# Fourier mixing and gated MLP in fp32: another place for one low part, one shift and eight turns, with more buffers for turns and outgoing rows

## The chip, the cores and the metric

The kernel runs on one core of a Trainium2 chip. The metric is device microseconds (us) of one execution; the time before is 964.4 us, the median of three runs.

## The reference

`x` is 2048 rows of 512, in fp32. All weights are given in fp32. `mod` is six vectors of 512 made from a condition `c`.

```python
sa, ca, ga, sb, cb, gb = (silu(c) @ w_mod) in six parts
h = layernorm(x) * (1 + ca) + sa
a, b = h @ dft_hid_re.T, h @ dft_hid_im.T
x = x + ga * (dft_seq_re @ a - dft_seq_im @ b)
h = layernorm(x) * (1 + cb) + sb                 # called h2 below
z = gelu(h @ w_in)                               # 512 -> 1792
z1, z2 = z[:, :896], layernorm(z[:, 896:])
out = x + gb * ((z1 * (w_sp @ z2 + b_sp)) @ w_out)
```

## The kernel before

**Three products for one.** Every fp32 matrix product is made of three products of a faster type: high part by high part, high by low, low by high (`matmul3`, L95 to L97). So each operand is split: ScalarE (ACT) copies the high part, VectorE (DVE) subtracts it to get the low part. For a moving block number n these are `prep_hi` (tile `ah`, L249) and `prep_lo` (tile `al`, L265). TensorE (PE) can't begin block n before `ah` n, nor its low product before `al` n. There are four buffers of `ah`, three of `al` and two of `t`, the block before the split.

**Stage 1**, blocks n = 0 to 127. A block is 128 x 512 of a sequence DFT matrix, loaded by SyncE (SP, L155) and turned on DVE (`squares`, L186). `mm_a(n)` does twelve matmuls with it against the 16 held row blocks of `h`. The blocks come in four groups t of 32; a group gives 512 output rows. Every 16 blocks four sums are split (`gh` on ACT L90, `gl` on DVE L91). Group t's sums go through the hidden DFT in four `mm_y(t, i)` of 24 matmuls, i = 0 to 3, each 128 rows. After each come:

- `post_y(t, i)`: DVE multiplies by `ga` (L546), adds x (L547), takes statistics (L103, L105); GpSimd (POOL) stores the rows (L548) and works out scale and shift (L107, L108, L115).
- `norm_y(t, i)`: ACT applies them (L119), which gives `h2`.
- `post_h(t, i)`: DVE multiplies by `1 + cb` (L557), POOL adds `sb` (L558).
- `turn_h(t, i)`: DVE turns 32 x 32 squares into a tile `hturn` (L564), of which there is one; POOL then issues four DMAs (L567) that write it to `ht_d[t]` in HBM.

**Stage 2a**, n = 128 to 155 (N2 = 128), makes the first half of `z` from `ht_d` by seven products of a Strassen-like scheme, two blocks n at a time (`mm_z1`, at even n). Its moving blocks lie in `xb` (groups 0 and 1 of `ht_d`, loaded near the end of stage 1) and `tt` (groups 2 and 3, loaded by SP at L205, at n = N2 and N2 + 3). Results are copied on ACT (`empty_z1`, L704) or finished with a gelu on ACT and a store by POOL (`end_z1`, L666 and L669) from rows `z1o`, of which there are three. **Stage 2b**, from N3 = 156, does the same for the second half (`mm_z2`, products emptied by DVE L742 and ACT). Then comes the long product with `w_sp` (`mm_w`, PSUM tiles `gw`), and the last one.

**Beside these**, blocks of `w_sp` are loaded (`load_s`, SP L761), summed on DVE in two steps one n apart (`sum_s`, L766 and L767, then L770 and L771) and stored (POOL L774) as operands of the long product.

**What sets the order.** Every engine runs its instructions in the order in which the program issues them. The program goes through n; before the block's matmuls `prep(n)` issues `ah` of n + 3 and `al` of n + 2, and behind them `run(n)` issues what `at(n, f, ...)` has put there by hand. So an `ah` stands behind all that ACT was given up to then, and so on. The last group's rows (t = 3) have no matmuls behind them in stage 1: their work is all put at N2 - 0.25, row after row, mixed with the first splits of the weights (`hi_v`, `lo_v`, `make_w7`, L606 and L614) and, ahead of row 2, with `prep(N2)`. Behind them `change_s()` closes the pools of stage 1 and opens `slots` in their place. Blocks n with n % 4 == 3 have their `al` in such a slot from N2 on, so `al` 131 (the low part of block N2 + 3) is issued after all turns of the last group.

```python
        if n % 2 == 0:
            prep_lo(n + 3)
        run(n)
        if n % 2 == 0:
            mm_z1(n)
```

Of the kernel before, what the change touches and what calls it, by code (L numbers as in the profile page):

```python
# [8 lines left out]
F32 = mybir.dt.float32  # L9
F32R = mybir.dt.float32r  # L10
AF = mybir.ActivationFunctionType
ALU = mybir.AluOpType

P = 128
# [5 lines left out]
def fnet_gmlp_kernel(  # L20
# [32 lines left out]
    nc = tc.nc  # L53
    S, D = x.shape[1:]
    F2 = w_in.shape[1]
    FH = F2 // 2
    Q = 512
    NQ = S // Q
# [7 lines left out]
    def pool(name, side="left", bufs=1):  # L66
        return tc.tile_pool(name=name, bufs=bufs, side=side, reuse_waits="tile")
# [55 lines left out]
    def at(n, f, *a):  # L123
        fill.setdefault(n, []).append((f, a))
# [14 lines left out]
    N2 = 4 * len(src)  # L139
    YPROD = (1, 2, 6, 7, 4, 5, 3)  # L140
    NY = {p: N2 + 4 * i for i, p in enumerate(YPROD)}
    N3 = N2 + 4 * len(YPROD)
# [7 lines left out]
    stage, T, AH, AL = {}, {}, {}, {}  # L150
# [39 lines left out]
    def prep(n):  # L190

        if n not in prepared:
            prepared.add(n)
            prep_hi(n + 3)
            prep_lo(n + 2)

    def slot(i, name, dtype=F32):
        return slots[0].tile([P, Q], dtype, tag=f"slot{i}", bufs=1, name=name)

    slots, TT, S2, XH = [], {}, {}, {}  # L200
# [55 lines left out]
    def prep_lo(n):  # L256
        if n >= NE or n in lows:
            return
        lows.add(n)
        if N2 <= n < N4 and n % 4 == 3:  # L260
            AL[n] = slot(0, f"al{n}", F32R)
        else:
            AL[n] = blocks.tile([P, Q], F32R, tag="al", bufs=3, name=f"al{n}")
        t = T.pop(n)
        nc.vector.tensor_tensor(AL[n], t, AH[n].bitcast(F32), op=ALU.subtract)  # L265
        gg, kk = divmod(n % 4, 2)
        if NY[6] <= n < NY[6] + 4:
            nc.vector.tensor_tensor(TT[kk, gg], TT[kk, gg], S2[gg, kk], op=ALU.add)
        elif NY[7] <= n < NY[7] + 4:
            nc.vector.tensor_tensor(TT[2 + kk, gg], TT[2 + kk, gg], S2[gg, kk], op=ALU.subtract)  # L270
# [4 lines left out]
    rows = p2.enter_context(pool("rows", "right"))  # L275
    s1 = ctx.enter_context(ExitStack())
    spool = s1.enter_context(pool("spool", "right"))
    GP_ = []
# [13 lines left out]
    wm, mods = {}, {}  # L292
# [262 lines left out]
    def post_h(t, i):  # L555
        h2 = LN.pop((t, i))
        nc.vector.tensor_tensor(h2, h2, mods[4], op=ALU.mult)  # L557
        nc.gpsimd.tensor_tensor(h2, h2, mods[3], op=ALU.add)  # L558
        LN[t, i] = h2

    def turn_h(t, i):
        h2 = LN.pop((t, i))
        ht = GP_[0].tile([P, D], F32, tag="hturn", bufs=1, name=f"hturn{t}_{i}")
        nc.vector.transpose(ht.rearrange("p (b i) -> p b i", i=32), h2.rearrange("p (b i) -> p b i", i=32))  # L564
        v = ht_d[t].rearrange("(b c) (a i r) -> a i c b r", c=32, a=4, i=4)
        for a in range(4):
            nc.gpsimd.dma_start(v[a, i], ht[32 * a:32 * a + 32].rearrange("c (b r) -> c b r", r=32))  # L567


    ZT = {}  # L570
# [76 lines left out]
    def mm_f7(g, k, th, tl):  # L647

        if k == 0:
            ZT["f7", g] = bank(6 + g % 2, f"f7p{g}")  # L650
        matmul3(ZT["f7", g], W7[0][:, 0, k], W7[0][:, 1, k], th, tl, k == 0, k == ND - 1)
        if k == ND - 1:
            end_z1(g, NF - 1, ZT.pop(("f7", g)), out_row(g, NF - 1))

    def out_row(g, f, tag="z1o"):
        return zrow[0].tile([P, Q], F32, tag=tag, bufs=3 if tag == "z1o" else 6, name=f"z1o{g}_{f}")

    def natural(z):
        return z.rearrange("p (a k i) -> p k a i", a=4, i=32)
# [39 lines left out]
    def empty_z1(p, gg, f):  # L699

        ps = ZT[gg, f]
        if p in (1, 6, 7):
            Z1[p, gg, f] = zrow[0].tile([P, Q], F32, tag="z1u" if p == 6 else "z1m", bufs=6, name=f"z1_{p}_{gg}{f}")
            nc.scalar.activation(natural(Z1[p, gg, f]), turned(ps), AF.Copy)  # L704
        elif p in (2, 4):
            g, f = gg, f + (3 if p == 4 else 0)
            end_z1(g, f, ps, out_row(g, f, "z1u" if p == 2 else "z1o"))
        else:
            z = Z1.pop((7 if p == 5 else 6, gg, f))
            nc.vector.tensor_tensor(natural(z), turned(ps), natural(z), op=ALU.add)  # L710
            end_z1(2 + gg, f + (3 if p == 5 else 0), None, z)
# [233 lines left out]
    norm_x(1)  # L945
    lo_h(0)
    prep_lo(0)
    hi_h(1)
    prep_hi(1)
    stats_x(2)  # L950
    lo_h(1)
    prep_lo(1)
    norm_x(2)
    prep_hi(2)
# [40 lines left out]
    for j, turn, weigh, row, fold, hi in ((0, (25, 26, 27, 28), (29, 29, 30, 30), 26, (34, 34, 35, 36), (38, 35, 36, 37)),  # L995
# [8 lines left out]
        n = weigh[3] + (3 if j == 0 else 1)  # L1004
# [4 lines left out]
            at(hi[k], make_ht, j, k)  # L1009
            at(hi[k] + 1, make_ht_lo, j, k)  # L1010
    for j, load_at, n, m, k, plus_one in ((2, 41, 49, 50, 7, False), (4, 52, 56, 58, 7, True),
                                          (3, 60, 65, 66, 7, False), (5, 68, 74, 76, 6, False)):
        at(load_at, load_mod, j)
        at(n, sum_mod, j, [0, 1])
        at(m, sum_mod, j, [2, 3])
        at(m + 1, split_mod, j)
        at(m + 3, spread_mod, j, k, cpool if j == 5 else htpool, plus_one)
    for t in range(NQ):
        n = 8 * NQ * (t + 1)
        for i in range(4):  # L1020
            y = N2 - 1 if t == NQ - 1 else (54, 56, 58, 60)[i] if t == 0 else n + (7, 9, 11, 13)[i] if t == 1 else n + 1 + 3 * i
            if i < 2:
                at(y - 4, load_xr, t, i)
            if t == 0:
                at((41, 42, 43, 45)[i], mm_y, t, i, (0,))
                at((42, 43, 44, 46)[i], keep_y, t, i)
            at(y, mm_y, t, i, (0, 1) if t else (1,))
            if t < NQ - 1:
                at(y + 1, post_y, t, i)
                at(y + 2, norm_y, t, i)  # L1030
                at(y + 3 if t else 71 + i, post_h, t, i)
                at(y + 4 if t else 72 + 2 * i, turn_h, t, i)
                if i < 2:
                    at(y + 2 if t else y + 3, load_xr, t, i + 2)
            else:
                if i == 2:
                    at(N2 - 0.25, prep, N2)
                at(N2 - 0.25, post_y, t, i)
                at(N2 - 0.25, norm_y, t, i)
                if i:  # L1040
                    at(N2 - 0.25, turn_h, t, i - 1)
                at(N2 - 0.25, post_h, t, i)
                if i < 2:
                    at(N2 - 0.25, load_xr, t, i + 2)
                for f, *a in (((hi_v, 1), (lo_v, 1)), ((make_w7, 0),), ((hi_v, 2), (lo_v, 2), (make_w7, 1)), ((turn_h, t, 3),))[i]:
                    at(N2 - 0.25, f, *a)
# [8 lines left out]

    wstack = ctx.enter_context(ExitStack())
    w0 = ctx.enter_context(ExitStack())
    wpool, zpool, zrow, bpool, spre, gpool = [], [], [], [], [], []
    at(N2 - 0.5, change_w)
    def change_s():  # L1060
        p2.close()
        slots.append(ctx.enter_context(pool("slots", "right")))
        spre.append(ctx.enter_context(pool("spre", "right")))
        bpool.append(ctx.enter_context(pool("bpool", "right")))
# [3 lines left out]
        spre.append(hp.enter_context(pool("spre0")))  # L1068

    at(80, change_q)  # L1070
    when = [(82 + 4 * i, 3) for i in range(11)] + [(N2 + 6, 8), (N2 + 14, 8), (N2 + 22, 8), (N3 + 4, 6), (N3 + 10, 6)]
    for (n, m), u in zip(when, ((r, g, b) for g in range(2) for b in range(4) for r in range(2))):
        at(n, load_s, *u)
        at(n + m, sum_s, *u, True)
# [6 lines left out]
        run(n + 0.75)  # L1081

    change_s()
    at(N2, load_t, 2)
    at(N2 + 1, load_wi, 1, 0)
    at(N2 + 1, load_wi, 1, 2)
# [35 lines left out]
    for i, p in enumerate(PROD):  # L1122
        for k in range(8):
            n = NB[p] + 2 * k
# [10 lines left out]
    for f in range(NF):  # L1135
        n = N4 + 24 + 8 * f
# [107 lines left out]
```

## Time and profile before

| | |
|---|---|
| median of 3 runs | 964.4 us (963.7 to 964.64) |
| profiled execution, its own time | 961.22 us |
| its span, first to last instruction | 959.4 us |
| mean granted TensorE clock | 0.992 |
| instructions | 12378 |
| PE, DVE, ACT, POOL busy | 936.5, 738.0, 413.6, 204.4 us |

The profile is one execution. A busy time is the sum over an engine's instructions; an engine that is not busy waits for another engine, for a DMA, or has nothing left. In a timeline row the first number is the start, the second the duration (of all, where x3 or x4 stands), and a bracket at its end gives the idle time of the engine ahead of it and who ended it. `Lnn` is the line in the kernel before. In the changed kernel the same lines stand 2 to 4 lines lower from L564 on (L564 is L565, L567 is L569, L666 is L670, L704 is L708, L742 is L746).

### The profile page before, as it was taken

The page shows a single profiled execution, that of the slowest core. Times are in us where ns is not written, and L with a number is a line of the kernel's source. Part 1 is how long each engine was busy: PE and PEld are TensorE (multiplying, and loading weights), DVE is VectorE, ACT ScalarE, POOL GpSimd, SP SyncE. Part 2 cuts the span into 40 slices and gives each one's busy share as a digit, 9 for nine tenths or more (in the row PEclk, how much of TensorE's full clock was granted, in tenths as well). Part 3 has the DMA queues.
Part 4 walks back from the last instruction along what each step waited for, and adds up shares of the span by engine and source line. Part 5 has one row for each costly group of instructions (what it writes and reads, how often), then busy time and mean ns, then how long its engine had stood idle before and what let it go on. Part 6 is the DMA issues. An engine that isn't in the chain of part 4 may idle for free.

```text
span 959.4 us, 12378 instructions
## 1 busy us (share of the span) xinstructions
PE 936.5 (98%) x4114; PEld 774.2 (81%) x4114; DVE 738.0 (77%) x1197; ACT 413.6 (43%) x725; POOL 204.4 (21%) x378
## 2 busy tenths in 40 slices
PE   8999999999999999999599999999999999999998
PEld 5888888888877888888487898788888888888886
DVE  7799957785668677866586859999799889886662
ACT  4694424232132221321485867766545454332221
POOL 2330000113663165325513301332000000000000
PEclk9999999999999999999799999999999999999999
DMA  9996652666348977994575413453465455744451
GB/s 210 220 222 131 128 141 62 172 176 154 107 119 238 320 215 211 279 333 160 185 268 197 198 44 88 112 152 88 111 142 138 105 135 123 192 92 161 178 178 61
DMA packets 235600, 157.07 MB, mean 164 GB/s; under 512 B 130448, under 2 KB 202384, under 8 KB 235408
## 3 DMA queue, kind: packets, MB, share of 16 engines
q1 hardware_dynamic: 223008, 118.65, 49.8%
q0 software_dynamic: 12192, 37.24, 10.9%
q8 instruction: 32, 0.52, 0.2%
q10 hardware_dynamic: 336, 0.39, 0.1%
q14 instruction: 32, 0.26, 0.1%
HBM read 119.54 MB, written 36.70 MB: 163 GB/s over the span
## 4 chain that ended last, share of the span: by engine, by line
PE 48%; DVE 2%; ACT 1%; POOL 1%; DMA 1%; issue 1%; DVEq 0%; POOLq 0%; ACTq 0%
PE gw L97 10%; PE gw L95 9%; PE gw L96 9%; PE op L95 3%; PE op L96 3%; PE op L97 3%; PE z1p L96 2%; PE z1p L97 2%; PE z1p L95 2%; PE z2p L97 2%; PE z2p L96 2%; PE z2p L95 2%; DMA ht_d<-hturn 1%; DVE al L265 1%; DVE z L742 0%
## 5 line engine op out<-in xcount | busy, mean ns | idle before, releaser
L249 ACT ACTIVATE ah<-t 128x512 fp32r<-128x512 f32 x248 | 156.4, 631 | 373.3 <-DVE t L186 259.6
L265 DVE TENSOR_TENSOR al<-t,ah 128x512 fp32r<-128x512 f32 x248 | 167.4, 676 | 64.0 <-PE gp L96 38.0
L95 PE MATMUL gp<-ah,hh 128*128 128x512 f32 x496 | 193.7, 391 | 2.4 <-DVE gl L91 2.4
L96 PE MATMUL gp<-al,hh 128*128 128x512 f32 x496 | 193.8, 391 | 1.7 <-DVE al L265 1.7
L97 PE MATMUL gp<-ah,hl 128*128 128x512 f32 x496 | 193.5, 390 | 0.0
L186 DVE STREAM_TRANSPOSE t<-stage 128x512 f32<-128x512 f32 x240 | 168.7, 703 | 8.4 <-DMA stage<-in_A_dft_seq_re_dram 3.6
L97 PE MATMUL gw<-ah,bl 128*128 128x512 f32 x400 | 155.8, 390 | 0.3 <-DVE bl L802 0.3
L95 PE MATMUL gw<-ah,bh 128*128 128x512 f32 x400 | 155.7, 389 | 0.0
L96 PE MATMUL gw<-al,bh 128*128 128x512 f32 x400 | 155.6, 389 | 0.0
L95 PEld LDWEIGHTS gp<-ah,hh 128*128 128x128 f32 x496 | 93.4, 188 | 22.4 <-DVE gl L91 2.8
L96 PEld LDWEIGHTS gp<-al,hh 128*128 128x128 f32 x496 | 93.5, 188 | 21.5 <-DVE al L265 2.2
L97 PEld LDWEIGHTS gp<-ah,hl 128*128 128x128 f32 x496 | 93.6, 189 | 19.4
L97 PEld LDWEIGHTS gw<-ah,bl 128*128 128x128 f32 x400 | 75.1, 188 | 16.5 <-DVE bl L802 1.0
L96 PEld LDWEIGHTS gw<-al,bh 128*128 128x128 f32 x400 | 75.1, 188 | 15.6
L95 PEld LDWEIGHTS gw<-ah,bh 128*128 128x128 f32 x400 | 75.1, 188 | 15.5
L774 POOL DMA_DIRECT2D s_d<-sj x64 | 35.2, 550 | 114.3 <-DVE sj L766 97.5
L95 PE MATMUL yp<-hth,gh 128*128 128x512 f32 x128 | 49.8, 389 | 0.0
L96 PE MATMUL yp<-htl,gh 128*128 128x512 f32 x128 | 49.8, 389 | 0.0
L97 PE MATMUL yp<-hth,gl 128*128 128x512 f32 x128 | 49.8, 389 | 0.0
L567 POOL DMA_DIRECT2D ht_d<-hturn x64 | 42.2, 665 | 31.1 <-DVE hturn L564 25.9
L95 PE MATMUL op<-woh,uh 128*128 128x512 f32 x112 | 43.6, 389 | 0.0
L96 PE MATMUL op<-wol,uh 128*128 128x512 f32 x112 | 43.6, 389 | 0.0
(199 smaller groups left out, 1451.0 us busy)
## 6 DMA issues: line engine op xcount, KB each, us to landing
stage<-in_A_dft_seq_im_dram SPq DMA_DIRECT2D x64, 256.0 KB, 5.1
sj<-in_B_w_sp_dram SPq DMA_DIRECT2D x32, 512.0 KB, 7.4
s_d<-sj POOLq DMA_DIRECT2D x64, 256.0 KB, 4.1
stage<-s_d SPq DMA_DIRECT2D x128, 128.0 KB, 2.8
stage<-in_A_dft_seq_re_dram SPq DMA_DIRECT2D x60, 256.0 KB, 5.5
stage<-in_B_w_sp_dram SPq DMA_DIRECT2D x96, 128.0 KB, 3.1
wm<-in_w_mod_dram SPq DMA_DIRECT2D x16, 256.0 KB, 5.6
xr<-in_A_x_dram POOLq DMA_DIRECT2D x16, 256.0 KB, 4.4
```

Source lines behind the costliest of these rows:

```text
L95: nc.tensor.matmul(acc, ah, bh, start=first, stop=False, skip_group_check=go_on)
L96: nc.tensor.matmul(acc, ah, bl, start=False, stop=False, skip_group_check=go_on)
L97: nc.tensor.matmul(acc, al, bh, start=False, stop=last, skip_group_check=go_on)
L186: nc.vector.transpose(dst.rearrange("p (b i) -> p b i", i=32), block[:, :, 32 * k:32 * k + 32])
L249: nc.scalar.activation(AH[n], T[n], AF.Copy)
L265: nc.vector.tensor_tensor(AL[n], t, AH[n].bitcast(F32), op=ALU.subtract)
L567: nc.gpsimd.dma_start(v[a, i], ht[32 * a:32 * a + 32].rearrange("c (b r) -> c b r", r=32))
L774: nc.gpsimd.dma_start(s_d[m, r, g][b * P:(b + 1) * P, :], a)
```

## The change

There are seven edits.

1. `al` 131 is issued inside the last group's rows, behind `post_y(3, 3)`, and lies in a buffer of the ring `z1u` (six rows of the pool `z1rows`) instead of a slot.
2. `sb` is added on DVE instead of POOL for the last group.
3. Turns (3, 1) and (3, 3) go into buffers of the ring `row` (six) instead of the one `hturn`.
4. Of turn (3, 3)'s four DMAs the last two are issued by ACT.
5. The rows `z1o` get a pool of their own with seven buffers, instead of three.
6. The vector `sb` (mod 3) is summed at n = 63 and 64 instead of 65 and 66; `post_h(0, i)` stands at 68 + i instead of 71 + i; the turns of group 0 stand at 69, 71, 73, 75 instead of 72, 74, 76, 78, those of group 1 at 77, 80, 82, 84 instead of 75, 77, 79, 81.
7. The last five `load_s` stand at N2 + 6, 14, 20, 26 and 32, each with its sums 8 and 9 behind, instead of N2 + 6, 14, 22 (8 and 9 behind) and N3 + 4, N3 + 10 (6 and 7 behind).

```diff
         if N2 <= n < N4 and n % 4 == 3:
-            AL[n] = slot(0, f"al{n}", F32R)
+            AL[n] = slot(0, f"al{n}", F32R) if slots else zrow[0].tile([P, Q], F32R, tag="z1u", bufs=6, name=f"al{n}")
...
     def post_h(t, i):
-        nc.gpsimd.tensor_tensor(h2, h2, mods[3], op=ALU.add)
+        (nc.vector if t == NQ - 1 else nc.gpsimd).tensor_tensor(h2, h2, mods[3], op=ALU.add)
...
     def turn_h(t, i):
-        ht = GP_[0].tile([P, D], F32, tag="hturn", bufs=1, name=f"hturn{t}_{i}")
+        pl, tag, n = (rows, "row", 6) if t == NQ - 1 and i % 2 else (GP_[0], "hturn", 1)
+        ht = pl.tile([P, D], F32, tag=tag, bufs=n, name=f"hturn{t}_{i}")
...
-            nc.gpsimd.dma_start(v[a, i], ht[32 * a:32 * a + 32].rearrange("c (b r) -> c b r", r=32))
+            eng = nc.scalar if (t, i) == (NQ - 1, 3) and a > 1 else nc.gpsimd
+            eng.dma_start(v[a, i], ht[32 * a:32 * a + 32].rearrange("c (b r) -> c b r", r=32))
...
     def out_row(g, f, tag="z1o"):
-        return zrow[0].tile([P, Q], F32, tag=tag, bufs=3 if tag == "z1o" else 6, name=f"z1o{g}_{f}")
+        if tag == "z1o":
+            return zout[0].tile([P, Q], F32, tag=tag, bufs=7, name=f"z1o{g}_{f}")
+        return zrow[0].tile([P, Q], F32, tag=tag, bufs=6, name=f"z1o{g}_{f}")
...
-                                          (3, 60, 65, 66, 7, False), (5, 68, 74, 76, 6, False)):
+                                          (3, 60, 63, 64, 7, False), (5, 68, 74, 76, 6, False)):
...
-                at(y + 3 if t else 71 + i, post_h, t, i)
-                at(y + 4 if t else 72 + 2 * i, turn_h, t, i)
+                at(y + 3 if t else 68 + i, post_h, t, i)
+                at(y + 4 if t > 1 else (69 + 2 * i, (77, 80, 82, 84)[i])[t], turn_h, t, i)
...
                 at(N2 - 0.25, post_y, t, i)
+                if i == 3:
+                    at(N2 - 0.25, prep_lo, N2 + 3)
                 at(N2 - 0.25, norm_y, t, i)
...
-    when = [(82 + 4 * i, 3) for i in range(11)] + [(N2 + 6, 8), (N2 + 14, 8), (N2 + 22, 8), (N3 + 4, 6), (N3 + 10, 6)]
+    when = [(82 + 4 * i, 3) for i in range(11)] + [(N2 + d, 8) for d in (6, 14, 20, 26, 32)]
...
     change_s()
+    zout.append(w0.enter_context(pool("zout")))
```

**Around `al` 131 on DVE**, at the end of stage 1. The rows of before start with the last row's `post_y(3, 3)`; `h2_3_3` is its `h2`, and the number behind a name only tells buffers apart.

```order
L546 TENSOR_TENSOR y3_3_4220<-yp3_3_0_4099,mod2_1784 128x512
L547 TENSOR_TENSOR xr3_3_4183<-y3_3_4220,xr3_3_4183 128x512
L103 BN_STATS bsty_4224<-xr3_3_4183 128x6
L105 BN_AGGR mvy_4226<-bsty_4224 128x2
L564 STREAM_TRANSPOSE hturn3_2_4235<-h2_3_2_4205 128x512
L557 TENSOR_TENSOR h2_3_3_4233<-h2_3_3_4233,mod4_2060 128x512
L564 STREAM_TRANSPOSE hturn3_3_4243<-h2_3_3_4233 128x512
L265 TENSOR_TENSOR al131_4261<-xb0_3845,ah131_4188 128x512
L265 TENSOR_TENSOR al132_4312<-xb1_3935,ah132_4305 128x512
```

The same place on DVE in the changed kernel:

```order
L546 TENSOR_TENSOR y3_3_4220<-yp3_3_0_4099,mod2_1784 128x512
L547 TENSOR_TENSOR xr3_3_4183<-y3_3_4220,xr3_3_4183 128x512
L103 BN_STATS bsty_4224<-xr3_3_4183 128x6
L105 BN_AGGR mvy_4226<-bsty_4224 128x2
L265 TENSOR_TENSOR al131_4233<-xb0_3845,ah131_4188 128x512
L565 STREAM_TRANSPOSE hturn3_2_4237<-h2_3_2_4205 128x512
L557 TENSOR_TENSOR h2_3_3_4235<-h2_3_3_4235,mod4_2060 128x512
L558 TENSOR_TENSOR h2_3_3_4235<-h2_3_3_4235,mod3_2222 128x512
L565 STREAM_TRANSPOSE hturn3_3_4245<-h2_3_3_4235 128x512
L265 TENSOR_TENSOR al132_4315<-xb1_3935,ah132_4308 128x512
```

`al` 131 moved up past both turns and the multiplication between them, and one addition (L558) came in ahead of the last turn.

**On ACT at the same place**, in the changed kernel; before, the same rows stand there without the DMAs:

```order
L119 ACTIVATE h2_3_3_4235<-xr3_3_4183,nmry_4231,rsy_4228 128x512
L569 DMA ht_d3_83<-hturn3_3_4245 32x16x32 x2
L708 ACTIVATE z1_1_00_4302<-z1p1_00_4274 128x4x4x32
L708 ACTIVATE z1_1_01_4304<-z1p1_01_4281 128x4x4x32
L708 ACTIVATE z1_1_02_4306<-z1p1_02_4288 128x4x4x32
L249 ACTIVATE ah132_4308<-xb1_3935 128x512
L249 ACTIVATE ah133_4313<-xb1_3935 128x512
```

The two DMAs stand ahead of three copies of a product (L708) and of `ah` 132, the high part that PE needs first for the pair N2 + 4.

**On DVE in stage 1**, around n = 80. Before, with `t` and `al` the blocks' turns and low parts, `gl2_0` the low parts of the sums:

```order
L186 STREAM_TRANSPOSE t82_2666<-stage20_2341 128x512
L265 TENSOR_TENSOR al81_2670<-t81_2627,ah81_2629 128x512
L91 TENSOR_TENSOR gl2_0_0_2685<-gp2_0_0_2141,gh2_0_0_2684 128x512
L91 TENSOR_TENSOR gl2_0_1_2689<-gp2_0_1_2142,gh2_0_1_2688 128x512
L91 TENSOR_TENSOR gl2_0_2_2693<-gp2_0_2_2143,gh2_0_2_2692 128x512
L91 TENSOR_TENSOR gl2_0_3_2697<-gp2_0_3_2144,gh2_0_3_2696 128x512
L564 STREAM_TRANSPOSE hturn1_2_2705<-h2_1_2_2600 128x512
L186 STREAM_TRANSPOSE t83_2713<-stage20_2341 128x512
L265 TENSOR_TENSOR al82_2722<-t82_2666,ah82_2668 128x512
L557 TENSOR_TENSOR h2_1_3_2711<-h2_1_3_2711,mod4_2060 128x512
L186 STREAM_TRANSPOSE t84_2746<-stage21_2530 128x512
L265 TENSOR_TENSOR al83_2750<-t83_2713,ah83_2715 128x512
```

In the changed kernel, from behind `gl2_0` on:

```order
L186 STREAM_TRANSPOSE t83_2701<-stage20_2359 128x512
L265 TENSOR_TENSOR al82_2710<-t82_2660,ah82_2662 128x512
L565 STREAM_TRANSPOSE hturn1_1_2728<-h2_1_1_2503 128x512
L557 TENSOR_TENSOR h2_1_3_2699<-h2_1_3_2699,mod4_2060 128x512
L186 STREAM_TRANSPOSE t84_2740<-stage21_2536 128x512
L265 TENSOR_TENSOR al83_2744<-t83_2701,ah83_2703 128x512
L186 STREAM_TRANSPOSE t85_2758<-stage21_2536 128x512
L265 TENSOR_TENSOR al84_2762<-t84_2740,ah84_2742 128x512
L565 STREAM_TRANSPOSE hturn1_2_2776<-h2_1_2_2600 128x512
L186 STREAM_TRANSPOSE t86_2785<-stage21_2536 128x512
L265 TENSOR_TENSOR al85_2789<-t85_2758,ah85_2760 128x512
L186 STREAM_TRANSPOSE t87_2803<-stage21_2536 128x512
```

Turn (1, 1) now comes behind `gl2_0` where (1, 2) came, and (1, 2) and (1, 3) follow two blocks apart each, instead of (1, 3) alone.

More of the change, by code (lines that the diff above doesn't have):

```diff
@@ L1057, in fnet_gmlp_kernel @@
     w0 = ctx.enter_context(ExitStack())
-    wpool, zpool, zrow, bpool, spre, gpool = [], [], [], [], [], []
+    wpool, zpool, zrow, zout, bpool, spre, gpool = [], [], [], [], [], [], []
     at(N2 - 0.5, change_w)
```

## Prediction

> **What bounds the kernel now.** I read the page's busy times first, then the waits of PE, then PE's timeline around each wait.
>
> ```profile
> PE 936.5 (98%) x4114; PEld 774.2 (81%) x4114; DVE 738.0 (77%) x1197; ACT 413.6 (43%) x725; POOL 204.4 (21%) x378
> ```
>
> PE is busy for 98% of the span. No edit takes a matmul away, so all there is to gain or lose is PE's idle time and the slow clock that may follow it. The waits of PE (us in total, times, longest):
>
> ```profile
> PE z1p L96 <- DVE al L265: 9.7, 1, 9.7
> PE gp L95 <- DVE gl L91: 2.4, 1, 2.4
> PE gp L96 <- DVE al L265: 1.7, 1, 1.7
> ...
> PE z2p L95 <- ACT ah L249: 1.4, 1, 1.4
> ...
> PE f7p L95 <- ACT ah L249: 0.4, 1, 0.4
> ```
>
> Three places matter. **B**, the largest, is where stage 2a begins; PE's timeline there:
>
> ```profile
> 460.53 0.39 PE L95 MATMUL z1p<-ah,vj 128*128 128x512 f32 x1
> 470.59 0.80 PE L96 MATMUL z1p<-al,vj 128*128 128x512 f32 x1 [9.67 <-DVE al L265]
> 471.18 0.63 PE L97 MATMUL z1p<-ah,vj 128*128 128x512 f32 x1
> ...
> 474.30 0.40 PE L96 MATMUL z1p<-al,vj 128*128 128x512 f32 x1
> ...
> 476.82 0.39 PE L95 MATMUL f7p<-ah,w 128*128 128x512 f32 x1
> ```
>
> From 474.30 to 476.82 stand 11 steps from matmul to matmul: 0.229 us each, the normal pace. From 460.53 to 474.30 there are 10 steps, which at that pace take 2.3 and took 13.8: a loss of 11.5. Of it 9.7 is the wait and 1.8 the slower steps behind it (0.63 long in the row of 471.18, where the others are 0.39).
>
> **A** is in stage 1, around n = 80 and 86:
>
> ```profile
> 275.08 0.39 PE L97 MATMUL gp<-ah,hl 128*128 128x512 f32 x1
> 277.83 0.50 PE L95 MATMUL gp<-ah,hh 128*128 128x512 f32 x1 [2.35 <-DVE gl L91]
> ...
> 282.97 0.39 PE L95 MATMUL gp<-ah,hh 128*128 128x512 f32 x1
> ...
> 291.26 0.50 PE L96 MATMUL gp<-al,hh 128*128 128x512 f32 x1 [1.74 <-DVE al L265]
> ```
>
> From 275.08 to 282.97 are 16 steps: 7.9 instead of 3.7, a loss of 4.2, of which 2.35 is the wait and 1.6 the slow clock (0.25 or so is the restart). The second wait costs 1.74 and a restart, 2.0, with no slow steps behind it. A loses 6.2. **C** is the small rest in stage 2: the 0.4 and 1.4 of the list, with 0.2 and restarts beside the first, about 2.8.
>
> **B after the change.** What PE waits for is `al` 131, which ends a row of work on DVE:
>
> ```profile
> 450.30 1.78 DVE L265 TENSOR_TENSOR al<-xb,ah 128x512 fp32r<-128x512 f32 x1
> 452.01 0.68 DVE L546 TENSOR_TENSOR y<-yp,mod 128x512 f32<-128x512 f32 x1
> 452.72 1.07 DVE L547 TENSOR_TENSOR xr<-y,xr 128x512 f32<-128x512 f32 x1
> ...
> 458.53 2.03 DVE L614 TENSOR_TENSOR w<-w,w 128x256 fp32r<-128x256 f32 x1
> 460.48 0.68 DVE L546 TENSOR_TENSOR y<-yp,mod 128x512 f32<-128x512 f32 x1
> 461.19 0.69 DVE L547 TENSOR_TENSOR xr<-y,xr 128x512 f32<-128x512 f32 x1
> ...
> 462.65 0.18 DVE L105 BATCH_NORM_AGGREGATE mvy<-bsty 128x2 f32<-128x6 f32 x1
> ...
> 465.01 0.69 DVE L557 TENSOR_TENSOR h<-h,mod 128x512 f32<-128x512 f32 x1 [0.34 <-ACT h L119]
> 469.26 0.71 DVE L564 STREAM_TRANSPOSE hturn<-h 128x512 f32<-128x512 f32 x1 [3.55 <-DMA ht_d<-hturn]
> 469.89 1.85 DVE L265 TENSOR_TENSOR al<-xb,ah 128x512 fp32r<-128x512 f32 x3
> ```
>
> The last row's statistics end at 462.83, but `al` 131 stands behind two turns, the second of them held 3.55 us by the DMAs of the turn before, which still read the one `hturn`. Issued behind the statistics it would start there. But the addition now comes in on DVE for each of the rows 0 to 2 ahead of it: 3 x 0.73 us (0.69 as L557, and the step to the next). Against that, DVE instructions with two inputs are long wherever POOL's addition runs beside them:
>
> ```profile
> 458.97 1.29 POOL L558 TENSOR_TENSOR h<-h,mod 128x512 f32<-128x512 f32 x1
> ```
>
> L614 takes 2.03 beside this one (its sibling of the same size, with no POOL work beside it, should take a half of the 0.69 of a 512-wide one, some 0.4), `al` takes 1.78 against 1.85 / 3 = 0.62, and L547 takes 1.07 twice against 0.69. Lifted, these give back 1.6 + 1.1 + 0.4 + 0.4 = 3.5. All of them lie on a chain that passes through POOL and ACT, so not all of it arrives: bounds are 0 and 3.5, less 2.2 spent. I take nearly the upper end, since the longest two stand directly in DVE's row ahead of a `y`: `post_y(3, 3)` starts at 460.48 - 1.3 = 459.2. Its statistics end 2.35 later, at 461.55, and `al` 131 ends at 462.2. PE is ready for it at 460.92, so a wait of **1.3** is left of 9.67.
>
> A new wait is next. The pair N2 + 4 needs `ah` 132 from ACT after 20 more matmuls (470.59 to 476.82 in the rows above), 20 x 0.229 = 4.6 us later: at 466.8. ACT's rows there:
>
> ```profile
> 464.16 0.81 ACT L119 ACTIVATE h<-xr,nmry,rsy 128x512 f32<-128x512 f32 x1 [6.24 <-POOL nmry L115]
> 464.88 1.55 ACT L704 ACTIVATE z<-z1p 128x512 f32<-128x512 f32 x3
> 466.32 1.16 ACT L249 ACTIVATE ah<-xb 128x512 fp32r<-128x512 f32 x2
> ```
>
> L119 starts 1.33 after the statistics' end (464.16 - 462.83), so at 462.9, and ends at 463.7. DVE then multiplies, adds and turns, 0.7 + 0.73 + 0.71: turn (3, 3) ends at 465.85, with nothing to hold it, as its buffer is another. Only then can ACT issue its two DMAs, and the three copies and `ah` 132 stand behind them. What such a DMA costs on ACT only one group of rows shows:
>
> ```profile
> L376 ACTq DMA_DIRECT2D x<-in_A_x_dram x4: 429/442/443, 0.7 to 2.1; - x4
> ```
>
> That is 0.44 us for rows of another shape; on POOL one of these takes 0.67 (2.68 / 4, below). I take 0.44, and keep 0.67. The DMAs are out at 466.75, the copies at 468.3, `ah` 132 at 468.9: a wait of **2.1**, and 0.4 more for `al` 132 (0.62 behind it, against one step of PE). So 3.8 of waits, 0.5 of restarts, and the slow clock: the nearest wait, 2.35 us, brought 1.6, the one of 1.74 nothing. I count 1.6 once. B then loses 5.9 instead of 11.5: **5.6 gained**.
>
> [...]
>
> The other readers of the turns are not late. POOL issues the four DMAs of turn (3, 2) behind `al` 131 and then two of (3, 3):
>
> ```profile
> 464.96 2.68 POOL L567 DMA_DIRECT2D ht_d<-hturn  x4 [0.83 <-DVE hturn L564]
> ...
> 471.49 2.58 POOL L567 DMA_DIRECT2D ht_d<-hturn  x4 [2.56 <-DVE al L265]
> ```
>
> From 462.9 six of them end at 466.9, where before the last ended at 474.07. `tt` of group 3 is loaded behind that, so it comes some 7 us earlier than now.
>
> **A after the change.** DVE's turns are held by the DMAs of the turn before:
>
> ```profile
> 271.68 0.71 DVE L564 STREAM_TRANSPOSE hturn<-h 128x512 f32<-128x512 f32 x1 [3.51 <-DMA ht_d<-hturn]
> ...
> 289.33 0.71 DVE L564 STREAM_TRANSPOSE hturn<-h 128x512 f32<-128x512 f32 x1 [6.18 <-DMA ht_d<-hturn]
> ```
>
> The first hold, of 3.51, stands just ahead of the `gl` that PE waited 2.35 for. In the changed order turn (1, 1) stands behind them and (1, 0) three blocks ahead, as mod 3's earlier sum lets group 0 turn three blocks earlier. I take this wait and its slow clock as gone: 4.2. The price comes behind it: turns (1, 1), (1, 2), (1, 3) now stand two blocks apart, 24 matmuls or 5.5 us, and each takes four issues (2.7) and the landing. Two windows show the landing, the first at 251 to 255 us beside a block's load, the other at 261 to 264 without:
>
> ```profile
> ht_d<-hturn POOLq DMA_DIRECT2D x4, 64.0 KB, 5.9
> ```
> ```profile
> ht_d<-hturn POOLq DMA_DIRECT2D x4, 64.0 KB, 2.1
> ```
>
> So a turn follows the one before by 4.8 to 8.6 us against 5.5. Here, beside loads of blocks and of `w_sp`, the longer is the nearer: the second turn is held about 3.1, the third up to 6. A hold of 6.18 cost PE 1.74, so DVE runs some 4.4 ahead. The second's hold fits in that, nearly (0.3); the third finds DVE's lead regained and costs about 1.7 as now. With restarts A loses 2.5 instead of 6.2: **3.7 gained** (bounds 6.2, with short landings, and -1, if the third adds 2.4 and a slow clock).
>
> **C after the change.** ACT's gelu into `z1o` is held by the store of an earlier row, and DVE's sums of `w_sp` stand among the emptying of `z2p`:
>
> ```profile
> 517.16 0.60 ACT L666 ACTIVATE z1o<-z1p 128x512 f32<-128x512 f32 x1 [2.77 <-DMA z_d<-z1o]
> ```
> ```profile
> 576.91 0.68 DVE L766 TENSOR_TENSOR sj<-sj 128x512 f32<-128x512 f32 x1
> ```
>
> Seven buffers end the hold; PE's waits of 0.4 and 0.2 with their restarts, 1.0, go. Four sums of 0.7 move away from 577 to 582, four blocks earlier, where they stand beside the first products of stage 2b and may cost 0.4; of the 1.4 wait at the end I take 1.2 as gone. **1.8 gained**, between -0.5 and 2.8.
>
> **Sum.** 5.6 + 3.7 + 1.8 = 11.1 off the profiled execution's 961.2: 950.1. That execution lies 3.2 below the median of 964.4, so the forecast is 953.3 us.
>
> **The rivals.** *More is gained.* No slow clock at B (1.6), landings of 2.1 in A (2.5 more), C in full (0.5 more): 953.3 - 4.6 = 948.7. For it speaks that the wait of 1.74 brought no slow clock; against, that the landing beside a block's load was 5.9.
>
> *Less is gained.* The lifted holds pay nothing, since the chain through POOL and ACT sets the rows' pace, and the three additions stay: `post_y(3, 3)` at 462.7, `al` 131 at 465.7, a wait of 4.8 with a slow clock, then 0.9 for `ah` 132 and `al` 132, with restarts 7.8: 3.7 gained. If A's third turn queues at the same time, its gain is nothing, and so C's: 964.4 - 3.7 = 960.7. For it speaks that ACT's L119, which stands ahead of the multiplication, waits for POOL's constants (6.24 in its row), and not for DVE's room. If A loses its 1 besides, and C its 0.5, it ends near no change.
>
> *Slower.* ACT, in order, stands behind turn (3, 3): the turn's new buffer in `row` is the one that held `xr` of row (3, 2), and is free only when that row's store by POOL, among the loads, has landed. Each us that the turn ends later than 465.85 is a us on `ah` 132. The gains in A and C pay for 5.5 of them, B's for 5.6, and the bound of 0.2% is 1.9: from a turn at 478.9 on it is slower. At 481 the time is 953.3 + 15 = 968. Against it stands the row of that store's issue; the landing would have to take over 20 us:
>
> ```profile
> 454.09 0.56 POOL L548 DMA_DIRECT2D x_d<-xr  x1 [0.31 <-DVE xr L547]
> ```
>
> **Chances.** Forecast 0.58, more 0.18, less 0.18 (of which 0.05 within 0.2%), slower 0.06. A change of 0.2%, 1.9 us, is about what a measurement of this kernel can tell from none. So faster 0.89, within 0.2% 0.05, slower 0.06. The range reaches from 946.5 (below the better case, by C's and A's bounds) to 961.
>
> **What would show it.** Right: the wait of z1p L96 for `al` falls from 9.7 to 1 or 2; a new wait for `ah` of about 2 stands at the pair N2 + 4, with ACT's two DMA issues ahead of it; gp L95 for `gl` is gone from the list; the last hold of a turn by `ht_d` stays near 6 us, and gp L96 for `al` near 2. The 2.77 of `z1o` is gone. Wrong: if DVE's `y` of the last row starts at 462 or later, the lifted holds paid nothing; if turns (1, 2) and (1, 3) show holds over 8, A is worse than counted; if ACT idles beyond 478 for the last turn, the slower case holds.

## The result and the profile after

| | before | changed |
|---|---|---|
| median | 964.05 us, 4 runs (962.89 to 964.64) | 950.62 us, 4 runs (949.74 to 951.59) |
| profiled execution | 961.22 us | 949.74 us |

The ratio is 0.9862, 95% interval 0.9845 to 0.9879: 1.4% faster. The two profiled executions differ by 11.5 us, where the forecast had 11.1. Of all executions in this document one, of the run E10 below, is left out: it took 2437.94 us, where the nine others took 957.25 to 963.16.

The waits of PE in the changed kernel (us in total, times, longest):

```profile
PE f7p L95 <- ACT ah L249: 2.3, 1, 2.3
PE z2p L95 <- ACT ah L249: 1.7, 2, 1.4
...
PE z1p L96 <- DVE al L265: 1.0, 1, 1.0
PE gp L96 <- DVE al L265: 0.9, 1, 0.9
```

The 9.7 for `al` 131 is 1.0, the 2.4 for `gl` has left the list, and a new 2.3 for `ah` stands on top. PE's timeline at B:

```profile
455.86 0.39 PE L95 MATMUL z1p<-ah,vj 128*128 128x512 f32 x1
457.21 0.50 PE L96 MATMUL z1p<-al,vj 128*128 128x512 f32 x1 [0.96 <-DVE al L265]
...
461.69 0.39 PE L97 MATMUL f7p<-ah,w 128*128 128x512 f32 x1
464.39 0.49 PE L95 MATMUL f7p<-ah,w 128*128 128x512 f32 x1 [2.31 <-ACT ah L249]
465.11 0.79 PE L96 MATMUL f7p<-al,w 128*128 128x512 f32 x1 [0.23 <-DVE al L265]
465.70 0.63 PE L97 MATMUL f7p<-ah,w 128*128 128x512 f32 x1
...
468.58 0.40 PE L95 MATMUL z1p<-ah,vj 128*128 128x512 f32 x1
```

From 455.86 to 468.58 there are 30 steps. At 0.229 us they take 6.9; they took 12.7. B loses 5.9 (12.72 less 6.87), where it lost 11.5. Who made `ah` 132 late is read on DVE and then on ACT:

```profile
454.23 0.68 DVE L546 TENSOR_TENSOR y<-yp,mod 128x512 f32<-128x512 f32 x1
...
456.50 0.66 DVE L265 TENSOR_TENSOR al<-xb,ah 128x512 fp32r<-128x512 f32 x1
...
460.55 0.71 DVE L565 STREAM_TRANSPOSE hturn<-h 128x512 f32<-128x512 f32 x1
464.37 1.29 DVE L265 TENSOR_TENSOR al<-xb,ah 128x512 fp32r<-128x512 f32 x2 [3.10 <-ACT ah L249]
```
```profile
458.25 0.81 ACT L119 ACTIVATE h<-xr,nmry,rsy 128x512 f32<-128x512 f32 x1 [5.56 <-POOL nmry L115]
461.30 0.91 ACTq L569 DMA_DIRECT2D ht_d<-hturn  x2
462.25 1.57 ACT L708 ACTIVATE z<-z1p 128x512 f32<-128x512 f32 x3 [3.18 <-PE f7p L97]
463.69 1.16 ACT L249 ACTIVATE ah<-xb 128x512 fp32r<-128x512 f32 x2
```

ACT has nothing to do from 459.1 to 461.3. The bracket of the 462.25 row puts its 3.18 us of idle time down to PE, but the matmuls of that product were long done: the row above shows that two DMA issues stood ahead in ACT's order, and they started when the turn had ended at 461.26. `ah` 132 is the first of two at 463.69.

In A two turns are still held, and PE's wait behind the second is short:

```profile
285.70 0.71 DVE L565 STREAM_TRANSPOSE hturn<-h 128x512 f32<-128x512 f32 x1 [4.84 <-DMA ht_d<-hturn]
...
292.82 0.71 DVE L565 STREAM_TRANSPOSE hturn<-h 128x512 f32<-128x512 f32 x1 [3.92 <-DMA ht_d<-hturn]
```
```profile
294.75 0.50 PE L96 MATMUL gp<-al,hh 128*128 128x512 f32 x1 [0.91 <-DVE al L265]
```

### The profile page after: what moved, and what is told of

It is laid out like the page before. It is cut to its first block, busy times and chain, and to the rows that moved or that the text cites. A ratio compares the mean times of both kernels' runs of the same rounds, so it can differ in the third digit from the quotient of the medians.

```text
span 948.0 us, 12382 instructions
## 1 busy us (share of the span) xinstructions
PE 934.8 (99%) x4114; PEld 773.2 (82%) x4114; DVE 737.5 (78%) x1201; ACT 413.5 (44%) x725; POOL 196.2 (21%) x372
## 4 chain that ended last, share of the span: by engine, by line
PE 86%; issue 6%; POOL 3%; DVE 3%; ACT 1%; DMA 1%; SPq 0%; POOLq 0%; DVEq 0%
PE gp L96 12%; PE gp L95 12%; PE gp L97 12%; PE gw L97 10%; PE gw L96 10%; PE gw L95 10%; PE op L97 3%; PE op L96 3%; PE op L95 3%; PE yp L97 2%; PE yp L96 2%; PE yp L95 2%; PE z2p L97 2%; PE z2p L96 2%; PE z2p L95 2%
```

## The experiments

Each ratio is to the kernel before, run beside it on the same chip; the changed kernel's is 0.9862. The kernel before took 963.1 to 965.1 us (medians) beside the different groups of runs, so two changed kernels are compared by their ratios, of which 0.001 is 0.96 us. Where two profiles are compared "matmul by matmul", it is by the start of the same matmul in both.

| | edit | median us | ratio, 95% interval |
|---|---|---|---|
| E1 | without edit 4 (POOL issues the last turn's DMAs) | 947.22 | 0.9816 (0.9798 to 0.9833) |
| E2 | without edit 2 (addition on POOL) | 955.42 | 0.9898 (0.9881 to 0.9915) |
| E3 | without edit 1 (`al` 131 late) | 953.59 | 0.9887 (0.9868 to 0.9906) |
| E4 | without edit 6 (turns of groups 0 and 1) | 956.27 | 0.9908 (0.9892 to 0.9923) |
| E5 | without edit 5 (three rows `z1o`) | 952.79 | 0.9887 (0.9872 to 0.9902) |
| E6 | without edit 7 (late sums) | 950.15 | 0.9857 (0.9839 to 0.9874) |
| E7 | without edit 3 (one `hturn`) | 955.32 | 0.9915 (0.9899 to 0.9932) |
| E8 | E1, turns (1, 2), (1, 3) later | 944.87 | 0.9804 (0.9789 to 0.9819) |
| E9 | before with edit 1 alone | 957.75 | 0.9942 (0.9922 to 0.9962) |
| E10 | before with edit 6 alone | 959.17 | 0.9960 (0.9942 to 0.9978) |
| E11 | E8 without edit 7 | 944.60 | 0.9810 (0.9786 to 0.9834) |

### E1: the last turn's DMAs on POOL

```diff
-            eng = nc.scalar if (t, i) == (NQ - 1, 3) and a > 1 else nc.gpsimd
+            eng = nc.gpsimd
```

> Edit 4 undone alone: POOL issues all four DMAs of the last turn, so nothing on ACT waits for the turn. Theory (ACT, in order, held ah 132 back): ACT has its three copies and ah 132 done 2.2 us after L119, that is before PE asks for it; only al 132, behind the turn on DVE, is left, a wait of 0.2 or so. The wait of 2.3, the slow steps behind it and the restart go, 4.5 us in all: about 946 us. Rival (the last rows of h2 reach HBM in time only because two queues issue them): their last issue comes 1.3 us later, the load of group 3 with it, and its first reader on ACT holds the products behind it: PE gets a new wait at the second or third pair, and the time stays at 950 or is above.

By the ratios the kernel is 4.4 us faster than the changed one (3.4 by the medians). On ACT and DVE nothing of the product stands behind the turn any more:

```profile
459.31 0.81 ACT L119 ACTIVATE h<-xr,nmry,rsy 128x512 f32<-128x512 f32 x1 [5.55 <-POOL nmry L115]
460.03 1.55 ACT L708 ACTIVATE z<-z1p 128x512 f32<-128x512 f32 x3
461.47 1.15 ACT L249 ACTIVATE ah<-xb 128x512 fp32r<-128x512 f32 x2
```
```profile
461.61 0.71 DVE L565 STREAM_TRANSPOSE hturn<-h 128x512 f32<-128x512 f32 x1
462.25 1.25 DVE L265 TENSOR_TENSOR al<-xb,ah 128x512 fp32r<-128x512 f32 x2
```

`ah` 132 is made while the last turn is still to come, and the wait of 2.3 has gone; a wait of 0.3 further on, for a gelu of ACT, is new. The theory holds: matmul by matmul PE gains 4.6 us in B and gives 0.4 back at the new wait, so the two DMA issues on ACT, 0.91 us of ACT's own time, cost about 4 us through what stood behind them. The rival's wait for the load of group 3 isn't there. The profiled execution is only 2.4 us below the changed kernel's. In A, where the kernel is the same, PE waited 2.33 instead of 0.91, and the old wait of 1.44 near the end of stage 2b was followed by a slow spell, which cost 1.6:

```profile
588.07 0.58 PE L95 MATMUL z2p<-wj,ah 128*128 128x448 f32 x1
```

The same matmuls are 0.36 long ahead of the wait.

### E2: the addition on POOL

```diff
-        (nc.vector if t == NQ - 1 else nc.gpsimd).tensor_tensor(h2, h2, mods[3], op=ALU.add)
+        nc.gpsimd.tensor_tensor(h2, h2, mods[3], op=ALU.add)
```

> Edit 2 undone alone: the addition of the last group is on POOL again. Theory (POOL's additions make DVE's two-input instructions beside them longer, by more than the additions cost DVE): al and L616 take 1.8 and 2.0 us again instead of 0.69 and 0.42, the last row's y starts about 1.3 us later against PE, the wait for al 131 grows from 1.0 to about 2.3, and the turn of the last row waits for POOL's addition besides (1.3 against 0.7): 952 to 954 us. Rival (the rows' pace is set by the chain through POOL and ACT, the addition costs DVE 0.73 a row for nothing): the wait for al 131 goes to nothing, and the time is 949 or below.

```profile
448.45 1.78 DVE L265 TENSOR_TENSOR al<-xb,ah 128x512 fp32r<-128x512 f32 x1
...
456.67 2.03 DVE L616 TENSOR_TENSOR w<-w,w 128x256 fp32r<-128x256 f32 x1
...
466.84 0.71 DVE L565 STREAM_TRANSPOSE hturn<-h 128x512 f32<-128x512 f32 x1 [2.66 <-POOL h L558]
```
```profile
461.60 0.50 PE L96 MATMUL z1p<-al,vj 128*128 128x512 f32 x1 [2.53 <-DVE al L265]
...
470.65 0.72 PE L95 MATMUL f7p<-ah,w 128*128 128x512 f32 x1 [4.22 <-ACT ah L249]
```

By the ratios the kernel is 3.5 us slower than the changed one. With POOL's addition back, the two instructions take 1.78 and 2.03 again, and the wait for `al` 131 grows by 1.6: three additions on DVE, 2.2 us, cost less than what they lift. This `al` takes 0.69 in the changed kernel, where POOL adds nothing, and 1.78 here, as in the kernel before. There POOL's additions beside that `al`, beside the long L614 and in the last row, with DVE idle, are these:

```profile
451.43 1.80 POOL L558 TENSOR_TENSOR h<-h,mod 128x512 f32<-128x512 f32 x1
...
458.97 1.29 POOL L558 TENSOR_TENSOR h<-h,mod 128x512 f32<-128x512 f32 x1
...
467.66 1.27 POOL L558 TENSOR_TENSOR h<-h,mod 128x512 f32<-128x512 f32 x1
```

So the first of them is longer beside DVE as well. Which of the two waited isn't shown, since the addition's record starts 1.1 us behind that of `al`. Nor is every DVE instruction with two inputs long there, as the prediction's "wherever" has it: L546 at 452.01 lies within the first of these additions and takes 0.68, as it does at 460.48 with none beside it. The median lies above the 952 to 954 us that I had expected; what I missed is that POOL's addition for the last row also stands behind the four DMA issues of turn (3, 2), so the last turn is held 2.66 us, and through ACT's order `ah` 132 with it. (In this profile A, which edit 2 doesn't touch, costs 2.8 us more than in the changed kernel's: its wait was 2.19, with a slow spell behind it.)

### E3: `al` 131 behind the turns

```diff
                 at(N2 - 0.25, post_y, t, i)
-                if i == 3:
-                    at(N2 - 0.25, prep_lo, N2 + 3)
```

> Edit 1 undone alone: al 131 is made behind all turns, in a slot. Theory (the place of al 131 is what removes the wait): it is made when turn (3, 3) has ended, about 461.3 on the scale of the changed kernel where PE is ready at 456.3, a wait of 5 to 5.5 with a slow clock of 1.6; the wait for ah 132 behind it is gone by then. B loses 7.2 or more instead of 5.8: 952 to 953 us. Rival (the other edits did it, since the turns aren't held any more): no difference, 950.6. If the slot, which lies over the closed pools, also waits for the last turn's DMAs, the wait is 8 or more, and the time 955 to 957.

```profile
462.15 0.79 PE L96 MATMUL z1p<-al,vj 128*128 128x512 f32 x1 [5.31 <-DVE al L265]
```

The wait is 5.3, as the theory had it, and there is no other at B. So of the 9.7 before, the other edits take about 4.4, and the place of `al` 131 another 4.3, of which ACT's wait gives back 2.3: matmul by matmul B loses 2.0 more than in the changed kernel. By the ratios the kernel is 2.4 us slower, with intervals that overlap a little; it is the waits that tell.

### E4: the old turns of the first two groups

```diff
-                at(y + 3 if t else 68 + i, post_h, t, i)
-                at(y + 4 if t > 1 else (69 + 2 * i, (77, 80, 82, 84)[i])[t], turn_h, t, i)
+                at(y + 3 if t else 71 + i, post_h, t, i)
+                at(y + 4 if t else 72 + 2 * i, turn_h, t, i)
```

The place of mod 3's sum is undone as well.

> Edit 6 undone alone: the first two groups' shifts and turns stand where they did. Theory (the turn held ahead of gl is the cause of the first wait in A): the waits of 2.4 for gl, with its slow clock, and of about 1.7 for al are back, A loses 6.2 instead of 1.1: about 955.5 us. Rival (the gain in A is chance of DMA times): the waits differ from those of before by more than 1.5 us, and the time is within 951 to 953.

```profile
PE gp L96 <- DVE al L265: 3.5, 1, 3.5
PE f7p L95 <- ACT ah L249: 2.3, 1, 2.3
PE z2p L95 <- ACT ah L249: 1.7, 2, 1.4
PE gp L95 <- DVE gl L91: 1.5, 1, 1.5
```

Both waits are back, and by the ratios the kernel is 4.4 us slower than the changed one. The two turns are held as long as before (3.50 and 6.31 us, against 3.51 and 6.18), but the waits of PE have other sizes (1.5 and 3.5 instead of 2.4 and 1.7): PE comes to the first one 0.6 us later than before and `gl` 0.2 sooner, and no slow spell lies between the two in which DVE could catch up.

### E5: three outgoing rows

```diff
-            return zout[0].tile([P, Q], F32, tag=tag, bufs=7, name=f"z1o{g}_{f}")
+            return zout[0].tile([P, Q], F32, tag=tag, bufs=3, name=f"z1o{g}_{f}")
```

> Edit 5 undone alone: three outgoing rows z1o instead of seven. Theory (the hold of the gelu by the store of an earlier row put ah of the pair at N2 + 20 late): ACT shows a hold of 2 to 3 us by a store again, PE its two waits of 0.4 and 0.2 at the pair behind it: 1.0 more, about 951.6 us. Rival (hidden): no wait of PE comes back, 950.6 us.

```profile
507.45 0.60 ACT L670 ACTIVATE z1o<-z1p 128x512 f32<-128x512 f32 x1 [2.88 <-DMA z_d<-z1o]
```
```profile
PE f7p L95 <- ACT ah L249: 2.8, 2, 2.3
PE z2p L95 <- ACT ah L249: 2.2, 2, 1.4
...
PE f7p L96 <- DVE al L265: 0.4, 2, 0.2
```

The hold is back (2.88 us on ACT), the waits of 0.4 and 0.2 at the pair behind it too, and the first wait of stage 2b grows by 0.6 (the total of z2p goes from 1.7 to 2.2). Matmul by matmul these make 2.0 us of the 2.4 by which this kernel is slower than the changed one by the ratios; the intervals overlap a little, so here too it is the waits that tell.

### E6: the late sums

```diff
-    when = [(82 + 4 * i, 3) for i in range(11)] + [(N2 + d, 8) for d in (6, 14, 20, 26, 32)]
+    when = [(82 + 4 * i, 3) for i in range(11)] + [(N2 + 6, 8), (N2 + 14, 8), (N2 + 22, 8), (N3 + 4, 6), (N3 + 10, 6)]
```

> Edit 7 undone alone: the last loads and sums of w_sp stand late again. The forecast counted the sums between 577 and 582 as the cause of 1.2 of the wait near the end of stage 2b: by that the wait grows from 1.4 to 2.6 and the time to 951.4 us, since the wait of 0.24 at the start of stage 2b goes. Theory now (that wait comes of ACT's four copies and four gelus, each behind an addition of DVE, ahead of ah; the sums have nothing to do with it): the wait stays at 1.4, the one of 0.24 with its 0.2 of slower steps goes, 950.1 us.

```profile
584.35 0.47 PE L97 MATMUL z2p<-wj,al 128*128 128x448 f32 x1 [0.39 <-DVE al L265]
...
590.77 0.47 PE L95 MATMUL z2p<-wj,ah 128*128 128x448 f32 x1 [1.37 <-ACT ah L249]
```

The wait near the end of stage 2b is 1.37 with the sums late and 1.44 with them early. They never caused it. The changed kernel's ACT shows what stands ahead of `ah` there, eight copies and gelus of one product, the gelus each behind an addition on DVE:

```profile
587.79 0.53 ACT L748 ACTIVATE z2p<-z 128x448 f32<-128x448 f32 x1
588.26 0.56 ACT L749 ACTIVATE z<-z 128x448 f32<-128x448 f32 x1
588.73 1.14 ACT L249 ACTIVATE ah<-t 128x512 fp32r<-128x512 f32 x2
```

That these set the wait is read from the order alone, since no run takes them away. Edit 7 trades one wait of 0.4 in stage 2b (the first row above) for one of 0.24 at its start. Matmul by matmul, with the slower steps beside them, each costs 0.8: no difference that can be told.

### E7: one `hturn` for the last group

```diff
-        pl, tag, n = (rows, "row", 6) if t == NQ - 1 and i % 2 else (GP_[0], "hturn", 1)
+        pl, tag, n = (GP_[0], "hturn", 1)
```

> Edit 3 undone alone: the one hturn holds all turns of the last group. Theory (the last turn then waits until the DMAs of turn (3, 2) have read it): those are issued until 461.1 on the scale of the changed kernel, land 2.1 later, so turn (3, 3) starts near 463.3 instead of 460.55, and ah 132, behind its DMAs on ACT, is 2.7 later: the wait of 2.3 grows to 5.0, 953 to 954 us. Rival (the hold by DMAs was the mix with loads and not the buffer): a hold of under 1 us, 951 us.

```profile
464.08 0.71 DVE L565 STREAM_TRANSPOSE hturn<-h 128x512 f32<-128x512 f32 x1 [3.19 <-DMA ht_d<-hturn]
```
```profile
467.89 0.79 PE L95 MATMUL f7p<-ah,w 128*128 128x512 f32 x1 [5.48 <-ACT ah L249]
```

The last turn is held 3.19, and the wait for `ah` 132 grows by 3.2, to 5.48 (5.0 expected). A us of the last turn is a us of PE, as the slower rival of the prediction had it; only its turn was never late.

### E8 and E11: the turns of group 1 further apart

E8 is E1 with this line changed; E11 is E8 with the sums of E6.

```diff
-                at(y + 4 if t > 1 else (69 + 2 * i, (77, 80, 82, 84)[i])[t], turn_h, t, i)
+                at(y + 4 if t > 1 else (69 + 2 * i, (77, 80, 83, 87)[i])[t], turn_h, t, i)
```

> The kernel with POOL's four DMAs for the last turn, and turns (1, 2) and (1, 3) one and three blocks later, at n = 83 and 87: beside the run with POOL's DMAs this tells what is left of the wait in A. Theory (turns two blocks apart are held by the DMAs of the turn before, 4 to 5 us each, and DVE's lead is used up at the third): with three and four blocks between them, 8.2 and 10.9 us, no turn is held for more than 1 us, the wait of PE for al near 294, 0.9 to 2.3, goes: 1.1 to 2.5 us faster than with POOL's DMAs alone, 945 to 946. Rival (the wait there is of the blocks' loads, not the turns): the wait stays, and the time with it.

```profile
286.01 0.71 DVE L565 STREAM_TRANSPOSE hturn<-h 128x512 f32<-128x512 f32 x1 [2.71 <-DMA ht_d<-hturn]
...
296.09 0.71 DVE L565 STREAM_TRANSPOSE hturn<-h 128x512 f32<-128x512 f32 x1 [1.84 <-DMA ht_d<-hturn]
```

The wait of PE in A is gone, and E8, at 944.9 us, is faster than both kernels: 2.0% under before. The holds are shorter but not below 1 as I had expected: three and four blocks are still less than issue and landing take here. They cost nothing, since DVE's lead covers them. That E8 is faster than E1 too, the times alone don't tell, as their intervals overlap; matmul by matmul the wait that is gone from A is worth 2.6 us.

> The spread turns with POOL's four DMAs, and edit 7 undone besides. Theory (the early sums cost a wait of 0.24 and 0.4 in all, at the start of stage 2b, and give nothing): 0.4 faster than with the spread turns, 944.5 us. Rival (chance): the same within 0.5.

944.60 against 944.87: the same.

### E9 and E10: one edit alone

E9 is the kernel before with the two places of edit 1, E10 with those of edit 6, as in the diff of the change.

> The kernel before with edit 1 alone: al 131 behind post_y(3, 3), all else as it was. Theory (the place of al 131 is what removes the wait; the buffers, the addition and ACT's DMAs only shape the wait behind it): al 131 ends at 463.5 on the scale of before, a wait of 2.5 instead of 9.7; ah 132 is early, as ACT has no DMAs, but al 132 stands behind turn (3, 3), which POOL's addition and the DMAs hold until 469: a second wait of 1.5 to 2. B loses 5 to 6.5 instead of 11.5: 957.5 to 959.5 us. Rival (the edits need each other): the second wait is as long as what the first lost, 962 us or above.

```profile
466.05 0.50 PE L96 MATMUL z1p<-al,vj 128*128 128x512 f32 x1 [2.53 <-DVE al L265]
...
473.78 0.50 PE L96 MATMUL f7p<-al,w 128*128 128x512 f32 x1 [1.07 <-DVE al L265]
```

Edit 1 alone takes the wait from 9.7 to 2.5, with a second one of 1.1 for `al` 132 behind the last turn. B is then as well off as with all edits. The time is at 957.75, in the range, and 5.6 us below before by the ratio; matmul by matmul B gains 5.8.

> The kernel before with edit 6 alone: the shifts and turns of the first two groups spread out. Theory (A and B are paid one after the other, since PE is busy between them): A loses about 1.1 instead of 6.2, B stays at 11.5: 959 to 960 us. Rival (PE, sooner through A, only waits longer for the same DMAs in B): 963 us or above.

Edit 6 alone gains 3.9 us by the ratio (959.17 us, in the range), all of it in A, and leaves B's wait at 9.6. What PE gains in A it doesn't lose again in B.

## Why the prediction was right, point by point

- **B, 5.6 forecast, 5.6 measured.** The last `y` starts at 454.23 instead of 460.48, 6.2 earlier, while PE is ready for `al` 131 4.7 earlier (455.86 against 460.53): 1.6 are gained at B itself, where 1.3 was forecast. `al` 131 ends at 457.16; the wait is 1.0 (1.3 forecast), that for `ah` 132 is 2.3 (2.1), for `al` 132 0.2 (0.4), and the slow clock came. That it came is luck: in E4 and E5 the same wait brought none. The two choices that no row of the same kind carried, ACT's 0.44 for a DMA issue and the near upper end of what POOL's addition had held, came out at 0.45 and, by E2, right.
- **A, 3.7 forecast, 5.1 measured.** The wait for `gl` is gone with its slow clock. The wait for `al` is 0.9 and not 1.7 plus 0.3: the term mis-sized is the third turn's hold, 3.92 against "up to 6". The second's was 4.84 against 3.1. Over the eight profiles with the same turns of group 1 this wait is 0.91 to 2.33, so the forecast lies within what happens, and that the profile of the changed kernel drew the least is luck.
- **C, 1.8 forecast, 1.6 measured.** The part of the rows `z1o` held: 1.0 forecast, 1.4 matmul by matmul (E5; in E9, which has three rows, a store of such a row held ACT for 0.8 at most and PE didn't wait, so the hold depends on the times as well). The part of the sums, 1.2, was wrong: "Four sums of 0.7 move away from 577 to 582 ... of the 1.4 wait at the end I take 1.2 as gone". E6 shows 1.37 and 1.44. The sums stood 20 us ahead of the wait, and DVE idled between; ACT's row of copies and gelus stands there instead. What the sums did hold up is a wait of 0.39 for `al` at 594.81 in the kernel before (E6's first row is the same one), which the forecast's C leaves out: without it 0.9 is gained, of which 0.7 is lost at the start of stage 2b.
- **Sum.** 5.6 + 5.1 + 1.6 = 12.3 matmul by matmul; 0.5 of it is lost in the first 10 us and 0.3 behind the last matmul, where nothing was changed, which leaves the 11.5 of the two profiled executions. So the three terms are off by 0, 1.4 and 0.2, and the sum came nearer than its parts. The forecast of 953.3 is 2.7 above the median: 0.4 of that is the sum, and 2.3 come from the step to the median: the profiled execution lay 3.2 below the median before, and 0.9 below it after.
- **The rivals.** "Less is gained" fails with E2: the lifted holds did pay. "Slower" had the right mechanism (E1, E7) and a turn that was in time. Edit 4 of its own accord costs 4.4 us (by the ratios) of the 17.7 that the rest would gain: by ACT's order, not by the DMAs.
- **Slips that the result doesn't hang on.** The six issues on POOL can't end at 466.9, since the last two wait for the turn's end at 465.85 and take 1.3; in the changed kernel they ended 2.8 us behind the turn, and PE waited for none of it. In A the lower bound adds up to -0.3 by its own terms, not -1, and in "more" C in full would be 1.0 more, not 0.5.

## What to carry to other kernels

On an engine that runs in order, an instruction that waits costs what stands behind it, not its own length: two DMA issues of 0.45 us each, moved from a queue with nothing behind it to one that feeds PE, cost PE a wait of 2.3 us and, in two of four profiles, a spell of slow clock. Before moving work between engines, list the next three rows behind it on the engine that takes it. And before counting a wait as the price of some work nearby, look whether the engine idles between that work and the wait: then it isn't.

## What the runs showed of the hardware

In these profiles the length of a wait of PE alone doesn't tell whether the granted clock falls behind it. Over all 13, past the first 20 us, all six waits of PE from 3.5 to 9.67 us were followed by a spell of slow steps, of eleven waits between 2.19 and 2.64 seven were, and of 72 up to 1.8 us one (the 1.44 of E1, shown there). At one place, the wait for `ah` 132, 2.31 and 2.35 us were followed by slow steps in the changed kernel and E6, and 2.34 and 2.35 us were not in E5 and E4. E5's rows at that wait:

```profile
465.57 0.50 PE L95 MATMUL f7p<-ah,w 128*128 128x512 f32 x1 [2.34 <-ACT ah L249]
...
466.64 0.40 PE L97 MATMUL f7p<-ah,w 128*128 128x512 f32 x1
```

They are 0.50 and 0.40 long, where the changed kernel's at 465.11 and 465.70 are 0.79 and 0.63. The records of the granted clock tell the two apart. In the kernel before it falls from 1.00 to 0.50 at 279.37 and 463.69 and is back at 282.79 and 473.93: from one of these times to the next are 1, 53 and 3 times 3.413 us. In E9 it falls at 279.43, 293.08 and 467.16, 4 and 51 times 3.413 apart. So PE's time is divided here into stretches of that length, counted from such a change. The changed kernel's around the wait, and then E5's (start and end, length, PE's busy time, granted clock):

```profile
461.59:465.00 3.41, 0.98 (x4) 1.00 0.51 96
465.00:468.41 3.41, 3.30 (x8) 0.50 0.39 132
```
```profile
460.87:464.29 3.42, 2.36 (x11) 1.00 0.59 119
464.29:467.70 3.41, 1.91 (x7) 1.00 0.20 40
467.70:471.11 3.41, 3.41 (x17) 1.00 0.80 257
```

In the changed kernel the whole wait fell into one stretch, in which PE was idle for 2.4 us, and the clock was 0.50 in the next. In E5 a wait of the same length fell into two, 1.1 and 1.5 us in each, and the clock stayed at 1.00. In the profiles before, changed and E9, past the first 20 us, six stretches that began at full clock had 1.87 to 2.77 us of idle PE, and the clock fell at the end of each; eleven had 0.41 to 1.65, and it fell behind none of them. No limit is to be read from that: in E1 it fell behind a wait of 1.44, and in the changed kernel a wait of 1.44 at the same place, in a stretch with 1.49 of idle, brought no slow step. All this is read from the profiles after the fact; no run was made to test it, and what sets the clock isn't shown.

A slow spell in the profiles before, changed, E9 and E10 has 6 to 8 steps of about 0.43 us instead of 0.23, so it costs some 1.2 to 1.6.
